# Block sums queued by the product that reads them, one more expert by block products, accumulators that swap roles, and a split last store

## The chip, the cores and the metric

One core of a Trainium2 chip. The time is that of the device, in microseconds (us), for one execution; a kernel is run several times and its median is given. PE is TensorE, DVE VectorE, ACT ScalarE, SP SyncE, POOL GpSimd.

## The reference, cut to what matters

```python
# attention with 4 sink positions and a window of 128, batch 4, 8 heads, 768 positions, 64 wide
x = attn_out.transpose(0, 2, 1, 3).reshape(3072, 512)
# mixture of E = 4 experts, D = 512, F = 1024
p = domain_probs / (domain_probs.sum(-1, keepdims=True) + 1e-09)
for e in range(E):
    h = np.maximum(x @ w1[e], 0.0)
    out += p[:, e:e + 1] * (h @ w2[e])
```

Of the kernel before, what the change touches and what calls it, by code (L numbers as in the profile page):

```python
# [16 lines left out]
def kernel(  # L17
# [12 lines left out]
    nc = tc.nc  # L30

    B, H, S, D = q.shape
    NSINK = int(n_sink)
    WIN = int(window)
    E, Dm, F = moe_w1.shape
    Ntok, Dout = out.shape

    P = 128
# [19 lines left out]
    ]  # L58

    NGATE = 5  # L60
    START = {0: 1, 1: 2, 2: 3, 3: 3}
    ONACT = 1
    ONE = 2
    PAIR = 1
    BEHIND = 800
    BIASED = 1
    FAST = tuple(START)
    UNITS = ("P1", "P5", "P6", "P2", "P7", "P3", "P4")
# [74 lines left out]
    def join(n, done):  # L143

        got = []

        def part(at):
            got.append(at)
            if len(got) == n:
                done(max(got))  # L150
        return part
# [12 lines left out]
    def sp(*deps, issue=530, takes=600):  # L164
        t["sp"] = max([t["sp"], *deps]) + issue
        at = max(t["hw"], t["sp"] + 800)
        t["hw"] = at + takes + max(0.0, min(takes, t["sw"] - at))
        return t["hw"] + 900
# [693 lines left out]
    class Mixture:  # L862
# [170 lines left out]
        def tokens(self):  # L1033

            pairs = [x for x in PAIRS if any(self.is_fast(x[0], e) for e in FAST)]
            n = len(self.T)
            if n == len(pairs):
                return
            b, g = pairs[n]
            if n > 1 and any((*pairs[n - 2], e) not in self.finished for e in range(E)):  # L1040
                return
            at = max(xT_at.get((b, hp, g), 1e12) for hp in range(NHP))
            if at > t["pe"]:
                return
            x = xT[b, g]
            B11, B21, B12, B22 = x[:, 1, 0:2], x[:, 1, 2:4], x[:, 0, 0:2], x[:, 0, 2:4]
            T = sb.tile([P, 4, 2, P], BF16, name="T", tag="T", bufs=2)
            self.T[b, g] = {"P1": B11, "P2": B21, "P3": B22, "P4": T[:, 3], "P5": T[:, 0], "P6": T[:, 1], "P7": T[:, 2]}
            steps = [(T[:, 0], B12, B11), (T[:, 1], B22, T[:, 0]), (T[:, 2], B22, B12), (T[:, 3], B21, T[:, 1])]

            def run(engine):
                nc.vector.tensor_sub(*steps.pop(0))
                done = dve(G, rate=1.92)
                if steps:
                    later("dve", t["dve"], 1500, run)
                else:
                    self.T_at[b, g] = done
            later("dve", at, 2500, run)
# [77 lines left out]

        def chore(self):

            if self.chores:
                return False  # L1140

            def go(fn, slack):
                def run(engine):
                    self.chores -= 1
                    fn(engine)
                self.chores += 1
                later("dve", t["pe"], slack, run)
                return True

            if self.last:  # L1150
                b, g, e = u = self.last[0]
                if (b, g, "P2") not in self.products:
                    self.last.pop(0)

                    def form(engine):
                        H12 = self.H[b, g, e][:, 1, :, 0]
                        nc.vector.tensor_sub(H12, H12, self.S[b, g][1][:, e])
                        self.S4_at[u] = dve(QF * P, rate=1.92)
                    return go(form, 1500)
            if not self.waiting:  # L1160
                return False
            b, g, e = u = self.waiting[0]
            if any(x[:2] < (b, g) and x[2] == "P5" for x in self.products) or any(x[:2] < (b, g) for x in self.last):
                return False
            if (b, g) == PAIRS[0] and len(self.stored) < 2 * NG:
                return False
            self.waiting.pop(0)
            if (b, g) not in self.S:
                self.S[b, g] = [mo.tile([P, E, QF, P], BF16, name=f"S{i}", tag=f"wide{i}", bufs=1) for i in range(2)]
            H = self.H[b, g, e]  # L1170
            H11, H21, H22 = H[:, 0, :, 0], H[:, 0, :, 1], H[:, 1, :, 1]
            S = self.S[b, g]
            steps = [(nc.vector.tensor_add, S[0][:, e], H21, H22), (nc.vector.tensor_sub, H21, H11, H21),
                     (nc.vector.tensor_sub, S[1][:, e], S[0][:, e], H11)]

            def form(engine):
                x = steps.pop(0)
                x[0](*x[1:])
                at = dve(QF * P, self.stored[-1] if (b, g) == PAIRS[0] else 0.0, rate=1.92)
                if steps:  # L1180
                    go(form, 3000)
                else:
                    self.S_at[u] = at
                    self.last.append(u)
            return go(form, 3000)

        def operand(self, b, g, e, m):
            H = self.H[b, g, e]
# [4 lines left out]
        def product_ready(self):  # L1193
            if not self.products:
                return 1e12
            b, g, m = self.products[0]
            e = self.order_of(b, g)[self.piece]
            at = (self.H_at if m in ("P1", "P2") else self.S4_at if m == "P3" else self.S_at).get((b, g, e), 1e12)
            bank = int(m in ("P2", "P5", "P3"))
            if self.piece == 0:  # L1200
                at = max(at, acc_free[bank])
            if m == "P1" and self.piece == E - 1 and acc_free[1] > 1e11:
                at = 1e12
            return max(at, max(forms_at.values()) if sum(formed.values()) == 4 * E else 1e12)

        def order_of(self, b, g):
            return [x[2] for x in self.order if x[:2] == (b, g)]

        def emit_product(self):
            ready = self.product_ready()  # L1210
            b, g, m = self.products[0]
            self.done += QF * G
            self.credit = max(self.credit - QF * G, 0.0)
            bank = int(m in ("P2", "P5", "P3"))
            x = acc[bank][:, 0:G]
            e, k = self.order_of(b, g)[self.piece], self.piece
            for f in range(QF):
                nc.tensor.matmul(  # L1218
                    x, lhsT=self.operand(b, g, e, m)[:, f], rhs=forms[e][m][:, f],
                    start=(k == 0 and f == 0 and m in ("P1", "P5")), stop=(k == E - 1 and f == QF - 1), skip_group_check=True,  # L1220
                )
            end = pe(QF * G, ready, n=QF)
            self.piece = (k + 1) % E
            if m == CHAIN[-1]:
                if (b, g, e) in self.lent:
                    self.spare.append(self.lent.pop((b, g, e)))
                else:
                    self.live -= 1
            if k < E - 1:
                return  # L1230
            self.products.pop(0)
            if m == "P1":
                out_sb[b, g] = mo.tile([P, 2, Dout], FP32, name="osb", tag="osb", bufs=1)
                r = (b * NQB + 2 * g) * P
                def store(at):
                    nc.sync.dma_start(out=out[r + P:r + 2 * P, :], in_=out_sb[b, g][:, 1])
                    sp(at)
                self.C22[b, g] = join(2, store)
            o = out_sb[b, g]
            C11, C12, C21, C22 = o[:, 0, 0:G], o[:, 0, G:], o[:, 1, 0:G], o[:, 1, G:]  # L1240
            acc_free[bank], seeded = 1e12, acc_free[1]
            if m == "P1":
                acc_free[1] = 1e12

            def run(engine):
                if m == "P1":
                    nc.scalar.copy(out=acc[1][:, 0:G], in_=x)
                    acc_free[0] = acc_free[1] = act(G, seeded)
                elif m == "P3":
                    nc.vector.tensor_add(C12, C12, x)  # L1250
                    acc_free[1] = at = dve(G)
                    nc.sync.dma_start(out=out[r:r + P, :], in_=o[:, 0])
                    sp(at)
                elif m == "P7":
                    nc.vector.tensor_add(C22, C22, x)
                    acc_free[0] = at = dve(G)
                    self.C22[b, g](at)
                else:
                    nc.scalar.copy(out={"P2": C11, "P6": C12, "P5": C22, "P4": C21}[m], in_=x)  # L1259
                    acc_free[bank] = at = act(G)  # L1260
                    if m == "P4":
                        self.C22[b, g](at)
            r = (b * NQB + 2 * g) * P
            later("dve" if m in ("P3", "P7") else "act", end, 200, run)

        def second_ready(self):
            if not self.second:
# [179 lines left out]
```

## The kernel before: what the change touches

The kernel is one long static plan. While it is built, a small model of the engines' clocks picks, step by step, what PE does next, and puts the work of VectorE and ScalarE into a list with deadlines (`later(engine, ready, slack, run)`). The order so found is fixed; on the chip each engine runs its own list in that order and waits where it must.

Both layers of the mixture use a scheme with seven block products in place of eight (2x2 blocks). In the first layer an expert is "fast", from the batch that `START` names on: seven products of 8 matmuls with 128 columns, in place of 32 matmuls with 256 columns. In the second layer a pair of token blocks (256 tokens) passes seven products P1, P2, P6, P5, P7, P3, P4, each over all four experts (four pieces of four matmuls of 256 columns), into two PSUM accumulators.

```python
START = {0: 1, 1: 2, 2: 3, 3: 3}
...
# the T sums of a pair's tokens (operands of the first layer's products)
at = max(xT_at.get((b, hp, g), 1e12) for hp in range(NHP))
if at > t["pe"]:
    return
...
later("dve", at, 2500, run)
...
def chore(self):                       # block sums of H, operands of the second layer
    if self.chores:                    # one at a time
        return False
    ...
        return go(form, 1500)          # H12 -= S1, after P2 has read H12
    ...
    steps = [(tensor_add, S[0], H21, H22), (tensor_sub, H21, H11, H21),
             (tensor_sub, S[1], S[0], H11)]
    def form(engine):
        x = steps.pop(0)
        x[0](*x[1:])
        ...
        if steps:
            go(form, 3000)             # the next sum enters the list when this one has run
        else:
            self.S_at[u] = at          # P6, P5, P7 may be planned from here on
    return go(form, 3000)
...
bank = int(m in ("P2", "P5", "P3"))    # the others go to accumulator 0
...
def run(engine):
    if m == "P1":                      # seed: P2 adds onto a copy of P1
        nc.scalar.copy(out=acc[1][:, 0:G], in_=x)
    elif m == "P3":
        nc.vector.tensor_add(C12, C12, x); nc.sync.dma_start(...)   # upper row block
    elif m == "P7":
        nc.vector.tensor_add(C22, C22, x); self.C22[b, g](at)
    else:
        nc.scalar.copy(out={"P2": C11, "P6": C12, "P5": C22, "P4": C21}[m], in_=x)
        if m == "P4":
            self.C22[b, g](at)         # lower row block, stored once P7 and P4 are both in
```

The softmax here doesn't subtract the row's maximum and nothing guards it: scores larger than these inputs give would overflow.

## Time and profile before

| | before |
|---|---|
| median of three runs at first (range) | 375.38 us (375.17 to 375.82) |
| span of the profiled run | 373.0 us |
| PE, DVE, ACT busy | 363.2, 284.6, 153.1 us |
| loading of weights and first inputs, PE partly waiting | to about 68 us |
| batch 0, then the mixture of batches 1 to 3 beside attention | about 68 to 131 us, then to 357 us |
| the last pair alone | 356.6 to 369.6 us |

The lines are shown in the prediction.

### The profile page before, as it was taken

To read this page: it belongs to the slowest core of one execution; us is meant where nothing else is said; L and a number is where in the kernel's file an instruction comes from. 1 tells how busy PE (TensorE), PEld (TensorE's weight loads), DVE (VectorE), ACT (ScalarE), POOL (GpSimd) and SP (SyncE) were. 2 spreads that over 40 slices of the span, in tenths; PEclk is the share of its full clock that TensorE was granted. 3 is DMA by queue.
4 is the path that set the end of the run, shared out by engine and by line. 5 is a ranking of instruction groups with operands and counts; after the bars stand their busy time and mean duration, and the time that the engine had idled before them with its cause. 6 is when DMAs were issued, how large, how long until landed. Compare 5 with 4: busy or idle time off the path is not lost.

```text
span 373.0 us, 9781 instructions
## 1 busy us (share of the span) xinstructions
PE 363.2 (97%) x4084; PEld 300.8 (81%) x4096; DVE 284.6 (76%) x630; ACT 153.1 (41%) x396; POOL 71.5 (19%) x91
## 2 busy tenths in 40 slices
PE   7999999999999999999999999999999999999996
PEld 3575767667667788888987988899999999999975
DVE  5664997674553899778879789779899889899930
ACT  4854633676565226445336145543103222222110
POOL 8935112808131192001020000000000000000000
PEclk9999999999999999999999999999999999999999
DMA  9999999949999999117991023213002111110011
GB/s 166 156 190 198 210 211 180 151 28 119 137 128 212 158 136 133 30 70 75 169 133 55 5 65 77 44 42 86 16 31 72 30 44 58 31 59 2 2 56 58
DMA packets 110808, 35.63 MB, mean 96 GB/s; under 512 B 94260, under 2 KB 106132, under 8 KB 110764
## 3 DMA queue, kind: packets, MB, share of 16 engines
q0 software_dynamic: 77520, 17.31, 52.1%
q1 hardware_dynamic: 32188, 17.18, 20.7%
q8 instruction: 32, 0.52, 0.6%
q10 hardware_dynamic: 1056, 0.52, 0.5%
q14 instruction: 12, 0.10, 0.1%
HBM read 40.45 MB, written 6.34 MB: 125 GB/s over the span
## 4 chain that ended last, share of the span: by engine, by line
PE 75%; DMA 15%; POOL 3%; ACT 3%; DVE 2%; issue 1%; POOLq 0%; ACTq 0%; DVEq 0%
PE acc L1218 29%; PE hps L1001 18%; PE cps L1078 17%; DMA w<-in_moe_w_dram 13%; PE acc L1286 5%; PE sps L618 2%; PE od L684 2%; DMA xT<-onat 2%; POOL qkn L189 1%; ACT onat L723 1%; DMA qkn<-in_q_dram 1%; PE tr L512 1%; POOL w L267 1%; ACT aT L643 1%; PE od L677 1%
## 5 line engine op out<-in xcount | busy, mean ns | idle before, releaser
L1001 PE MATMUL hps<-xT,w 128*128 128x256 bf16 x864 | 107.0, 273 | 1.3 <-DMA w<-in_moe_w_dram 0.9
L1001 PEld LDWEIGHTS <-w 128*128 128x128 bf16 x864 | 82.0, 98 | 14.4 <-issue 2.0
L1218 PEld LDWEIGHTS <-H 128*128 128x128 bf16 x600 | 56.0, 98 | 7.6 <-issue 1.9
L643 ACT ACTIVATE aT<-sps 128x512 bf16<-128x512 f32 (+1 forms) x96 | 47.0, 574 | 31.3 <-PE sps L618 31.2
L723 ACT ACTIVATE onat<-od,R 128x64 bf16<-128x64 f32 x144 | 33.3, 331 | 39.7 <-DVE R L711 39.7
L1218 PE MATMUL acc<-w,H 128*128 128x256 bf16 x360 | 47.7, 273 | 1.0 <-ACT osb L1259 0.5
L1025 DVE SCALAR_TENSOR_TENSOR H<-hps,gates 128x512 bf16<-128x512 f32 x56 | 38.0, 686 | 12.4 <-PE hps L1001 12.2
L1286 PE MATMUL acc<-w,H 128*128 128x512 bf16 x180 | 43.6, 379 | 0.7 <-issue 0.2
L1078 PEld LDWEIGHTS <-w 128*128 128x128 bf16 x672 | 42.4, 98 | 1.9 <-issue 0.5
L254 POOL DMA_DIRECT2D vx<-in_v_dram x24 | 21.4, 902 | 75.6 <-PE od L684 65.9
L1259 ACT COPY osb<-acc 128x256 f32<-128x256 f32 x36 | 13.6, 384 | 52.8 <-PE acc L1218 51.9
L1097 DVE SCALAR_TENSOR_TENSOR H<-cps,gates 128x512 bf16<-128x512 f32 x48 | 32.8, 685 | 2.1 <-PE cps L1078 1.3
L1286 PEld LDWEIGHTS <-H 128*128 128x128 bf16 x192 | 18.3, 98 | 17.5
L1218 PE MATMUL acc<-wf,H 128*128 128x256 bf16 x240 | 31.9, 273 | 0.0
L1014 ACT ACTIVATE H<-hps 128x512 bf16<-128x512 f32 x35 | 20.9, 598 | 24.8 <-PE hps L1001 24.4
L1218 PEld LDWEIGHTS <-S 128*128 128x128 bf16 x288 | 27.0, 98 | 3.9 <-issue 1.1
L1106 ACT COPY cps<-cps 128x512 f32<-128x512 f32 x21 | 12.1, 576 | 42.2 <-PE cps L1078 40.6
L1298 DVE SCALAR_TENSOR_TENSOR osb<-acc,scale_t,osb 128x512 f32<-128x512 f32 x18 | 13.5, 749 | 16.8 <-PE acc L1286 15.3
L1078 PE MATMUL cps<-T,w 128*128 128x128 bf16 x336 | 25.6, 219 | 0.0
L1078 PE MATMUL cps<-xT,w 128*128 128x128 bf16 x336 | 25.3, 219 | 0.0
L189 POOL DMA_DIRECT2D qkn<-in_q_dram x22 | 20.0, 907 | 18.1 <-PE tr L512 9.3
L1078 PEld LDWEIGHTS <-vf 128*128 128x128 bf16 x360 | 22.5, 98 | 1.0 <-issue 0.2
(117 smaller groups left out, 525.1 us busy)
## 6 DMA issues: line engine op xcount, KB each, us to landing
w<-in_moe_w_dram POOLq DMA_DIRECT2D x7, 1024.0 KB, 18.9
out_dram<-osb SPq DMA_DIRECT2D x24, 256.0 KB
gates<-gate_rows SPq DMA_DIRECT2D x36, 128.0 KB
vx<-in_v_dram POOLq DMA_DIRECT2D x24, 128.0 KB, 6.0
qkn<-in_q_dram POOLq DMA_DIRECT2D x22, 128.0 KB, 6.2
qkn<-in_k_dram POOLq DMA_DIRECT2D x22, 128.0 KB, 6.1
w<-in_moe_w_dram POOLq DMA_DIRECT2D x2, 512.0 KB, 9.0
kraw<-in_k_dram ACTq DMA_DIRECT2D x2, 256.0 KB
```

What stands on the lines that cost most here:

```text
L189: nc.gpsimd.dma_start(out=both[:, i], in_=src[b, :, tb * P:(tb + 1) * P, :].rearrange("h p d -> p h d"),)
L254: nc.gpsimd.dma_start(out=vx[tb][:, :, 0:D], in_=v[b, :, tb * P:(tb + 1) * P, :].rearrange("h p d -> p h d"),)
L643: nc.scalar.activation(out=a[:, ph], in_=sps[ph][:, 0:w], func=AF.Exp, scale=scale)
L723: nc.scalar.mul(o[:, qi, hp, ph * D:(ph + 1) * D], od[:, qi, ph, 0:D], R[:, qi, ph])
L1001: nc.tensor.matmul(h[:, i].rearrange("p (q n) -> p q n", q=2), lhsT=w1_sb[e][:, db, fb * P:(fb + 1) * P], rhs=xT[b, g][:, :, db], start=(i ...
L1014: nc.scalar.activation(out=dst, in_=h, func=AF.Relu)
L1025: nc.vector.scalar_tensor_tensor(out=dst, in0=h, scalar=0.0, in1=gate, op0=ALU.max, op1=ALU.mult,)
L1078: nc.tensor.matmul(y[:, f], lhsT=A[:, d, f * P:(f + 1) * P], rhs=T[:, d], start=(m in ("P1", "P5") and f == 0 and d == 0), stop=(d == 1), ...
L1097: nc.vector.scalar_tensor_tensor(out=dst, in0=src, scalar=0.0, in1=gate, op0=ALU.max, op1=ALU.mult)
L1218: nc.tensor.matmul(x, lhsT=self.operand(b, g, e, m)[:, f], rhs=forms[e][m][:, f], start=(k == 0 and f == 0 and m in ("P1", "P5")), stop=(k ...
L1259: nc.scalar.copy(out={"P2": C11, "P6": C12, "P5": C22, "P4": C21}[m], in_=x)
L1286: nc.tensor.matmul(op, lhsT=H[:, fb // QF, fb % QF, s], rhs=w2_sb[e][:, fb, :], start=(fb == 0), stop=(fb == NFB - 1),)
```

## The change

Its intent: take one more expert by seven products in batch 1, where VectorE has some time left; let the extra VectorE work not delay the sums that a product needs; take ScalarE's copies out of PE's way at the end of the kernel; make the last store shorter. The diff, cut to its core (lines left out are not marked one by one):

```diff
-    START = {0: 1, 1: 2, 2: 3, 3: 3}
+    START = {0: 1, 1: 1, 2: 3, 3: 3}
+    CHORES = 3
@@ tokens
                 return
+            at = t["pe"]
@@ chore
-            if self.chores:
+            if self.chores >= CHORES:
                 return False
-                    return go(form, 1500)
+                    return go(form, self.until(b, g, e, "P3"))
-            steps = [(add, S[0], H21, H22), (sub, H21, H11, H21), (sub, S[1], S[0], H11)]
+            steps = [(add, S[0], H21, H22), (sub, S[1], S[0], H11), (sub, H21, H11, H21)]
-                    go(form, 3000)
+                    go(form, self.until(b, g, e, "P6 P7".split()[len(steps) == 2]))
-            return go(form, 3000)
+            return go(form, self.until(b, g, e, "P6"))
+        def until(self, b, g, e, m):
+            n = self.products.index((b, g, m)) * E + self.order_of(b, g).index(e) - self.piece
+            return max(0.0, n * QF * G / 2.4 - 1000.0)
@@ products
-            bank = int(m in ("P2", "P5", "P3"))
+            bank = int(m in ("P2", "P5", "P3")) ^ PAIRS.index((b, g)) % 2
+            final = (b, g) == PAIRS[-1]
-                    start=(... m in ("P1", "P5")), ...
+                    start=(... m in (("P1", "P5", "P2") if final else ("P1", "P5"))), ...
-                if m == "P1":
-                    nc.scalar.copy(out=acc[1][:, 0:G], in_=x)
+                if m == "P1" and not final:
+                    nc.scalar.copy(out=other, in_=x)
+                elif m == "P2" and final:
+                    nc.vector.tensor_add(C11, C11, x)      # P1 went to C11 by ScalarE
@@ stores of the last pair's lower row block
+                    if final: store(at, slice(G, Dout))     # C22, after P7
+                    if m == "P4" and final: store(at, slice(0, G))   # C21, after P4
```

More of the change, by code (lines that the diff above doesn't have):

```diff
@@ L1172, in chore @@
             S = self.S[b, g]
-            steps = [(nc.vector.tensor_add, S[0][:, e], H21, H22), (nc.vector.tensor_sub, H21, H11, H21),
-                     (nc.vector.tensor_sub, S[1][:, e], S[0][:, e], H11)]
+            steps = [(nc.vector.tensor_add, S[0][:, e], H21, H22), (nc.vector.tensor_sub, S[1][:, e], S[0][:, e], H11),
+                     (nc.vector.tensor_sub, H21, H11, H21)]
             def form(engine):
@@ L1198, in product_ready @@
             at = (self.H_at if m in ("P1", "P2") else self.S4_at if m == "P3" else self.S_at).get((b, g, e), 1e12)
-            bank = int(m in ("P2", "P5", "P3"))
+            bank = self.bank(b, g, m)
             if self.piece == 0:
                 at = max(at, acc_free[bank])
-            if m == "P1" and self.piece == E - 1 and acc_free[1] > 1e11:
+            if m == "P1" and self.piece == E - 1 and acc_free[1 - bank] > 1e11:
                 at = 1e12
@@ L1207, in order_of, with bank @@
             return [x[2] for x in self.order if x[:2] == (b, g)]
+        def bank(self, b, g, m):
+            return int(m in ("P2", "P5", "P3")) ^ PAIRS.index((b, g)) % 2
         def emit_product(self):
@@ L1213, in emit_product, with store @@
             self.credit = max(self.credit - QF * G, 0.0)
-            bank = int(m in ("P2", "P5", "P3"))
+            r = (b * NQB + 2 * g) * P
+            def store(at, c=slice(0, Dout)):
+                nc.sync.dma_start(out=out[r + P:r + 2 * P, c], in_=out_sb[b, g][:, 1, c])
+                sp(at)
+            bank = self.bank(b, g, m)
+            other = acc[1 - bank][:, 0:G]
+            final = (b, g) == PAIRS[-1]
             x = acc[bank][:, 0:G]
@@ L1219, in emit_product @@
                     x, lhsT=self.operand(b, g, e, m)[:, f], rhs=forms[e][m][:, f],
-                    start=(k == 0 and f == 0 and m in ("P1", "P5")), stop=(k == E - 1 and f == QF - 1), skip_group_check=True,
+                    start=(k == 0 and f == 0 and m in (("P1", "P5", "P2") if final else ("P1", "P5"))), stop=(k == E - 1 and f == QF - 1), skip_group_check=True,
                 )
@@ L1233, in emit_product @@
                 out_sb[b, g] = mo.tile([P, 2, Dout], FP32, name="osb", tag="osb", bufs=1)
-                r = (b * NQB + 2 * g) * P
-                def store(at):
-                    nc.sync.dma_start(out=out[r + P:r + 2 * P, :], in_=out_sb[b, g][:, 1])
-                    sp(at)
-                self.C22[b, g] = join(2, store)
+                self.C22[b, g] = join(2, lambda at: store(at))
             o = out_sb[b, g]
             C11, C12, C21, C22 = o[:, 0, 0:G], o[:, 0, G:], o[:, 1, 0:G], o[:, 1, G:]
-            acc_free[bank], seeded = 1e12, acc_free[1]
-            if m == "P1":
-                acc_free[1] = 1e12
+            acc_free[bank], seeded = 1e12, acc_free[1 - bank]
+            if m == "P1" and not final:
+                acc_free[1 - bank] = 1e12
             def run(engine):
-                if m == "P1":
-                    nc.scalar.copy(out=acc[1][:, 0:G], in_=x)
+                if m == "P1" and not final:
+                    nc.scalar.copy(out=other, in_=x)
                     acc_free[0] = acc_free[1] = act(G, seeded)
+                elif m == "P2" and final:
+                    nc.vector.tensor_add(C11, C11, x)
+                    acc_free[bank] = dve(G)
                 elif m == "P3":
                     nc.vector.tensor_add(C12, C12, x)
-                    acc_free[1] = at = dve(G)
+                    acc_free[bank] = at = dve(G)
                     nc.sync.dma_start(out=out[r:r + P, :], in_=o[:, 0])
@@ L1255, in run @@
                     nc.vector.tensor_add(C22, C22, x)
-                    acc_free[0] = at = dve(G)
-                    self.C22[b, g](at)
+                    acc_free[bank] = at = dve(G)
+                    if final:
+                        store(at, slice(G, Dout))
+                    else:
+                        self.C22[b, g](at)
                 else:
-                    nc.scalar.copy(out={"P2": C11, "P6": C12, "P5": C22, "P4": C21}[m], in_=x)
+                    nc.scalar.copy(out={"P1": C11, "P2": C11, "P6": C12, "P5": C22, "P4": C21}[m], in_=x)
                     acc_free[bank] = at = act(G)
-                    if m == "P4":
+                    if m == "P4" and final:
+                        store(at, slice(0, G))
+                    elif m == "P4":
                         self.C22[b, g](at)
-            r = (b * NQB + 2 * g) * P
-            later("dve" if m in ("P3", "P7") else "act", end, 200, run)
+            later("dve" if m in ("P3", "P7") or final and m == "P2" else "act", end, 200, run)
         def second_ready(self):
```

## The prediction

> **What bounds the kernel now.** I read the page first, then the table by stretches, the timeline of the matmul engine, the list of waits, and the last microseconds of all engines. The engine shares and the chain that ended last:
>
> ```profile
> PE 363.2 (97%) x4084; PEld 300.8 (81%) x4096; DVE 284.6 (76%) x630; ACT 153.1 (41%) x396; POOL 71.5 (19%) x91
> ...
> PE 75%; DMA 15%; POOL 3%; ACT 3%; DVE 2%; issue 1%; POOLq 0%; ACTq 0%; DVEq 0%
> ```
>
> A busy PE is not proof of a full PE, because ends are modelled. So I look at starts. In the chain, sixteen matmuls of 128x256 take 1.75 us and sixteen of 128x128 take 0.89 us:
>
> ```profile
> 178.96 1.75 PE hps L1001 x16
> ...
> 257.67 0.89 PE cps L1078 x16
> ```
>
> That is 109 and 56 ns from start to start, i.e. 256 and 128 columns at 2.4 GHz plus about 2.5 ns. Adding up the start-to-start distances of all matmuls on the timeline, I find hardly any time above this rate from 120 us on. The PE is full, and the kernel is as long as its column count, plus the load stage before 65 us (the DMA's 15% of the chain), plus a few real gaps. The gaps after 120 us in which PE waited for another engine are in the list of waits from 110 us on, three entries over 0.3 us in all:
>
> ```profile
> PE acc L1218 <- ACT osb L1259: 1.0, 2, 0.5
> ...
> PE acc L1218 <- ACT acc L1247: 0.4, 1, 0.4
> ```
>
> Two of the three are in the last pair of blocks, where no other work is left to fill them. The timeline of PE:
>
> ```profile
> 354.70 1.47 PE L1218 MATMUL acc<-wf,qkT 128*128 128x256 bf16 x12
> 356.63 1.91 PE L1218 MATMUL acc<-w,H 128*128 128x256 bf16 x16 [0.46 <-ACT osb L1259]
> 358.99 1.91 PE L1218 MATMUL acc<-w,H 128*128 128x256 bf16 x16 [0.45 <-ACT acc L1247]
> ```
>
> The bracket undercounts, since it starts at the modelled end. By starts: 354.70 + 12 x 0.109 = 356.01, and the next starts at 356.63, so 0.62 us is lost; 356.63 + 16 x 0.109 = 358.37, next at 358.99, 0.62 us again. The first is the last pair's P1, which wants the accumulator that P4 of the pair before has just filled (ScalarE must copy it out). The second is P2, which adds onto a copy of P1 that ScalarE writes from one accumulator into the other. The third gap is at 204.57 (the same kind of wait as the first: P5 wants the accumulator of P2, and ScalarE was late because of attention's scaling work); 0.7 us by starts.
>
> VectorE is the second engine. By stretches (the columns are busy PE, PEld, DVE, ACT, POOL):
>
> ```profile
> 120.00:150.00 30.00, 29.95 (x337) 24.48 (x335) 26.98 (x62) 12.66 (x39) 14.03 (x17) 1.00 1.55 138
> 150.00:180.00 30.00, 29.96 (x355) 26.39 (x353) 24.21 (x54) 13.86 (x41) 1.75 (x2) 1.00 0.42 64
> 180.00:210.00 30.00, 29.45 (x329) 25.49 (x327) 24.77 (x60) 12.51 (x42) 2.62 (x3) 1.00 0.76 101
> ...
> 300.00:330.00 30.00, 30.00 (x393) 28.15 (x392) 27.43 (x58) 6.67 (x14) 0.00 (x0) 1.00 0.13 39
> ```
>
> In batch 1 (about 120 to 190 us) VectorE has some 3 to 6 us free in each 30; in the last batch 2.6.
>
> **What the Trainium skill says.** The page "TensorE: Matmul & The Clock Gate", section "Wait — 56ns, not 53.3ns?", gives N / 2.4 GHz plus about 2.5 ns between the starts of warm matmuls; the 56 and 109 ns above agree. The same page's "Back-to-back issue gap" expects some 81 ns at 128 columns where each matmul has its own weight load; this trace has such pairs at 56 ns, so I take 56. "PSUM — Partial Sum Buffer", "The four PSUM rules", says that writes of ScalarE and VectorE don't touch the written-bits, so that a matmul without the start flag adds onto what such an engine wrote: that is the seed by which P2 waits for ScalarE's copy, and why a P2 with the start flag needs no copy. "VectorE: DVE Perf Modes", "What auto-detection actually checks", has two results a cycle for 16-bit tensors and one otherwise: here 417 ns for a 512-wide bf16 sum and 685 ns for a 512-wide operation on f32 in PSUM agree.
>
> **The change part by part.**
>
> *Expert 1 by seven block products already in batch 1* (three more fast units, 24 for 21). A slow unit has 32 matmuls of 256 columns: 32 x 109.1 = 3.49 us. A fast unit has 7 x 8 of 128: 56 x 55.8 = 3.12 us. It saves 0.37 us of PE each, 1.10 us for three. It costs VectorE two more f32 operations a unit (six of about 685 ns for four): 2 x 3 x 0.685 = 4.1 us, and ScalarE two copies of 570 to 590 ns a unit, 3.5 us. Both fall into 120 to 190 us, beside PE work; VectorE has about 11 us free there (10 us stretches of 7.5, 10.0, 9.5, 7.7, 8.2, 8.3, 6.9 busy). I count nothing for them on the path. The weight sums of expert 1 exist anyway: three of the four are built by 51 us already, and the fourth, at 182 us before, moves to the end of batch 0 on expert 1; 0.69 us of VectorE moves, none is added.
>
> *Sums queued by the product that reads them, up to three at once, P6's sum before P7's; a laxer deadline for the token sums.* The same instructions in another order: 36 x 4 sums of 417 ns. They let the evictions that PE or a PSUM slot waits for go first. Since PE waits for VectorE practically nowhere from 120 us on, the direct gain is nil; it is what makes room for the 4.1 us.
>
> *Accumulators swap by pair.* P1 of a pair no longer goes into the bank that P4 of the pair before has just left. At eight borders; at seven of them PE has other work and the timeline shows no gap, so they give nothing. At the last: 0.62 us.
>
> *The last pair without the seed.* P1 is copied to the output, P2 starts fresh, and VectorE adds it (one more 128x256 addition, 0.41 us, under the P6 and P5 matmuls). P6 needs P1's accumulator read out, which has P2's 1.75 us to be done. Gain: 0.62 us, all on the path, as the six products after it run without a gap to the end.
>
> *Last store split.* After the last matmul (369.63) come a copy of 0.37 us, the store and its completion:
>
> ```profile
> 369.66 0.37 ACT L1259 COPY osb<-acc 128x256 f32<-128x256 f32 x1 [4.87 <-PE acc L1218]
> 370.06 0.33 SPq L1236 DMA_DIRECT2D out_dram<-osb  x1
> ...
> 370.50:371.00 0.50, 0.00 (x0) 0.00 (x0) 0.00 (x0) 0.00 (x0) 0.00 (x0) 1.00 0.20 74
> 371.00:371.50 0.50, 0.00 (x0) 0.00 (x0) 0.00 (x0) 0.00 (x0) 0.00 (x0) 1.00 1.02 389
> 371.50:372.00 0.50, 0.00 (x0) 0.00 (x0) 0.00 (x0) 0.00 (x0) 0.00 (x0) 1.00 0.17 62
> ```
>
> The data itself takes (0.20 + 1.02 + 0.17) x 0.5 = 0.70 us of the 16 engines; the rest, of 2.9 us from issue to end, is fixed. "DMA: Bandwidth & Descriptors", "Anatomy of one DMA — SWDGE (gpsimd) path", likewise puts some 2 us a DMA down as fixed, mostly the write's receipt. Half the bytes saves up to 0.35 us; the packets shrink from 2 KB to 1 KB, so I take 0.3 us. The other half leaves 1.7 us earlier, beside P4.
>
> Sum: 1.10 + 0.62 + 0.62 + 0.30 = 2.64 us, 0.7% of 375.38, which gives 372.7.
>
> **The rivals.** First, VectorE becomes the bound in batch 1. For it: it is at 100% from 130 to 140 us, where the first fast unit, the last weight sums and the block sums meet, and three fast units more there delay every H behind them. Against it: 11 us are free in the 70 us, and the order of the work is planned by deadline. If it came true, half of the 4.1 us could show as PE gaps, and the time would be some 374.5. Second, ScalarE: two of the three gaps at the accumulators were ScalarE's lateness or latency, and 3.5 us more for it comes in just the batches where attention's exponentials and scalings are still running. A few more gaps like the one at 204.57, of 0.5 to 0.7 us, would make 373.5 to 374. Third, in the other direction: with the queue reordered and the whole static plan shifted, the gap at 204.57 may vanish, which gives 372.0. Fourth, the gaps at the end merely move: P6 or P3 could wait for sums, as PE arrives 1.2 us sooner. Against it: the last block sum ends at 356.1 and P6 began at 360.73; the four sums for P3 end at 361.35 and P3 began at 365.97. Both have slack of over 4 us.
>
> **Range and chances.** The four gains are counted from instructions and are safe within some 0.3 us together. What is unsafe is the replanned order of the middle, which I take as 1 us either way (one or two gaps of the 204.57 kind gained or lost), a little more upward than downward. Hence 371.5 to 374.0. Faster by 2% would need 367.9 us, and there are not 7.5 us of waits to win, as PE's column count stays; slower by 2% needs a new bound that the free time of VectorE speaks against.
>
> **What would show it right or wrong.** Right: 1001's matmuls fall by 96 (864 to 768) and 1078's rise by 168; ScalarE's seed copies 21 to 24; no bracket on the last pair's P1 and P2; P6's first matmul of the last pair 1.75 us after P2's; the end of the span some 2.6 us after the last store's issue. Wrong: new brackets at block products between 120 and 250 us naming VectorE or ScalarE, filler matmuls after 100 us, a VectorE that is full for 30 us and more with PE gaps in it, or a last pair that waits for sums.

## More of the kernel before

All runs told of here are fast: the granted TensorE clock, given by the profile as a share of full speed, was 0.995 or more in each.

The output tile of a pair (`osb`) has a single buffer.

## The result, and the profile after

The changed kernel took 372.38 us (372.10 to 372.55, 4 runs) against 375.60 us (375.17 to 376.00) in the same rounds: a ratio of 0.9914, 95% interval 0.9897 to 0.9931. A ratio is the mean time of one kernel's fast runs over that of the other's of the same rounds, so not quite the ratio of the medians. In later rounds, those of runs 9 to 12, the changed kernel took 371.51 us against 375.42 us (0.9904). It is within 2%, and inside the forecast range.

The engine shares and the chain of the changed kernel's page:

```profile
PE 360.5 (97%) x4155; PEld 299.7 (81%) x4167; DVE 286.8 (77%) x636; ACT 157.7 (43%) x402; POOL 71.7 (19%) x91
...
PE 85%; DVE 6%; DMA 4%; ACT 2%; issue 1%; ACTq 0%; DVEq 0%
```

PE has more matmuls (71 more weight loads) and less to do, as narrower ones took the place of wide ones. PE's waits of over 0.15 us for another engine's data from 110 us on, in the list of waits of the changed kernel; the waits for accumulators, 1.0 and 0.4 us in the prediction's lines, are down to 0.2 us, and a short one for attention's scaling stands at 201.7 us:

```profile
PE od L685 <- ACT onat L724: 0.3, 1, 0.3
...
PE acc L1234 <- ACT osb L1277: 0.2, 1, 0.2
```

The last pair in the timelines of PE and of ScalarE, changed kernel. P1 and P2 now run as one block of 32 without a gap, but P6 starts late: 354.67 + 32 x 0.109 = 358.16, and it started at 358.48. It waited for ScalarE's copy of P1, and that copy started at 358.06, 1.6 us after P1's end, because of a DMA:

```profile
354.67 3.66 PE L1234 MATMUL acc<-w,H 128*128 128x256 bf16 x32
358.06 0.37 ACT L1277 COPY osb<-acc 128x256 f32<-128x256 f32 x1 [2.81 <-DMA out_dram<-osb]
358.48 1.91 PE L1234 MATMUL acc<-wf,S 128*128 128x256 bf16 x16 [0.15 <-ACT osb L1277]
```

The DMA is the store of the pair before, which still reads the one output buffer. Before the change the first write into that buffer came after P2 (360.97 us), when the store had landed.

The end of the changed kernel, by stretches (the last three columns are PE's clock, the busy share of the DMA engines, GB/s): the last half store takes (0.66 + 0.11) x 0.5 = 0.39 us of the DMA engines, not 0.70.

```profile
367.81 0.33 SPq L1226 DMA_DIRECT2D out_dram<-osb  x1
...
368.50:369.00 0.50, 0.00 (x0) 0.00 (x0) 0.00 (x0) 0.00 (x0) 0.00 (x0) 1.00 0.66 229
369.00:369.50 0.50, 0.00 (x0) 0.00 (x0) 0.00 (x0) 0.00 (x0) 0.00 (x0) 1.00 0.11 33
369.50:370.00 0.50, 0.00 (x0) 0.00 (x0) 0.00 (x0) 0.00 (x0) 0.00 (x0) 1.00 0.00 0
```

Yet from that issue to the end of the span 3.0 us passed, against 2.9 before. What stood between is what SyncE does at the end: it goes through a list of nine pairs of semaphores, one after the other. These are its checks (instructions by line, cut to the time from the last store's landing on), first in the kernel before, from 371.9 to 372.2 us, then in the changed one, from 369.3 to 370.0 us:

```profile
L1442 SPq EVENT_SEMAPHORE  x1: 28/28/28, 372.1 to 372.1; - x1
```
```profile
L1461 SPq EVENT_SEMAPHORE  x8: 27/28/28, 369.5 to 369.9; - x8
```

In these traces the DMAs of SyncE hold the semaphores 99, 101, 103, 104, 106, 107, 108 and 109 in turn. Before, the last store happened to hold the last one of the list, so one check was left when it landed. The split makes one DMA more; the last store now holds number 99, the second of the list, and seven checks follow it (from 2.41 to 2.84 us after the start of the last matmul, 0.43 us).

Stage by stage, from starts of certain instructions in the traces (us). "Load": to the first turning of the inputs that come after the weights. "Batch 0": to the 1192nd weight load, up to which all kernels here give PE the same order. "Middle": to the last pair's P1. "Last pair": to the start of the last matmul. "Tail": to the end.

| kernel (profiled run) | load | batch 0 | middle | last pair | tail |
|---|---|---|---|---|---|
| before | 67.78 | 62.97 | 225.88 | 12.72 | 3.63 |
| changed | 68.28 | 62.58 | 223.81 | 12.43 | 3.75 |
| changed, once more | 67.17 | 62.02 | 223.80 | 12.29 | 3.75 |
| without expert 1 | 68.08 | 62.81 | 225.59 | 12.12 | 3.73 |
| with the old queue | 67.57 | 63.18 | 226.61 | 12.12 | 3.74 |
| only expert 1 | 69.11 | 63.14 | 226.51 | 12.72 | 3.63 |
| only the accumulators and the stores | 68.23 | 63.82 | 225.37 | 12.12 | 3.75 |
| own output tiles | 68.11 | 62.33 | 223.81 | 12.12 | 3.76 |
| one last store | 68.13 | 62.02 | 223.81 | 12.12 | 3.62 |
| half store from GpSimd | 68.11 | 62.27 | 223.81 | 12.33 | 3.34 |
| own tiles and GpSimd | 67.59 | 62.45 | 223.80 | 12.12 | 3.33 |
| one sum at a time | 67.63 | 62.46 | 228.50 | 12.12 | 3.74 |
| fixed deadlines | 68.08 | 62.71 | 225.08 | 12.12 | 3.75 |
| no swap | 67.07 | 62.24 | 224.28 | 12.11 | 3.75 |

The six traces whose plan has the same middle agree there within 0.01 us, and so does the tail by its kind. Load and batch 0, where DMA has a say, vary by 2.0 and 1.8 us over all traces. So middle, last pair and tail carry the argument, and the sum of the first two is what makes times scatter.

### The profile page after: what moved, and what is told of

The parts are those of the page before. It is cut to its first block, busy times and chain, and to the rows that moved or that the text cites. A ratio compares the mean times of both kernels' runs of the same rounds, so it can differ in the third digit from the quotient of the medians.

```text
span 370.8 us, 9949 instructions
## 1 busy us (share of the span) xinstructions
PE 360.5 (97%) x4155; PEld 299.7 (81%) x4167; DVE 286.8 (77%) x636; ACT 157.7 (43%) x402; POOL 71.7 (19%) x91
## 4 chain that ended last, share of the span: by engine, by line
PE 85%; DVE 6%; DMA 4%; ACT 2%; issue 1%; ACTq 0%; DVEq 0%
PE acc L1234 28%; PE hps L1002 20%; PE cps L1080 19%; PE acc L1305 9%; PE sps L619 3%; PE od L685 2%; DMA xT<-onat 2%; DMA kraw<-in_k_dram 2%; PE tr L513 1%; ACT aT L644 1%; PE od L678 1%; DMA out_dram<-osb 1%; DVE H L1026 1%; DVE aT L638 1%; DVE onat L715 1%
## 5 line engine op out<-in xcount | busy, mean ns | idle before, releaser
L1002 PE MATMUL hps<-xT,w 128*128 128x256 bf16 x768 | 95.6, 273 | 0.4 <-DVE H L1017 0.4
L1002 PEld LDWEIGHTS <-w 128*128 128x128 bf16 x768 | 72.3, 98 | 12.5 <-issue 2.9
L1080 PEld LDWEIGHTS <-w 128*128 128x128 bf16 x768 | 48.2, 98 | 2.0 <-issue 0.5
L1099 DVE SCALAR_TENSOR_TENSOR H<-cps,gates 128x512 bf16<-128x512 f32 x57 | 38.8, 687 | 2.1 <-PE cps L1080 1.2
L1026 DVE SCALAR_TENSOR_TENSOR H<-hps,gates 128x512 bf16<-128x512 f32 x44 | 30.2, 690 | 9.3 <-PE hps L1002 9.0
L1080 PE MATMUL cps<-T,w 128*128 128x128 bf16 x384 | 29.3, 219 | 0.0
L1080 PE MATMUL cps<-xT,w 128*128 128x128 bf16 x384 | 29.1, 219 | 0.0
L1108 ACT COPY cps<-cps 128x512 f32<-128x512 f32 x24 | 13.8, 575 | 33.1 <-PE cps L1080 31.0
L1080 PEld LDWEIGHTS <-vf 128*128 128x128 bf16 x432 | 26.9, 98 | 1.0 <-issue 0.3
```

The source lines that it names most:

```text
L1002: nc.tensor.matmul(h[:, i].rearrange("p (q n) -> p q n", q=2), lhsT=w1_sb[e][:, db, fb * P:(fb + 1) * P], rhs=xT[b, g][:, :, db], start=(i ...
L1026: nc.vector.scalar_tensor_tensor(out=dst, in0=h, scalar=0.0, in1=gate, op0=ALU.max, op1=ALU.mult,)
L1080: nc.tensor.matmul(y[:, f], lhsT=A[:, d, f * P:(f + 1) * P], rhs=T[:, d], start=(m in ("P1", "P5") and f == 0 and d == 0), stop=(d == 1), ...
L1099: nc.vector.scalar_tensor_tensor(out=dst, in0=src, scalar=0.0, in1=gate, op0=ALU.max, op1=ALU.mult)
L1108: nc.scalar.copy(out=tiles["Y"], in_=y)
```

## The experiments

Times of a run are compared with the kernel before in the same rounds (375.42 us in each case). All results were correct.

**1. Without expert 1** (`no_expert1`): the changed kernel with `START = {0: 1, 1: 2, 2: 3, 3: 3}`.

> The changed kernel with expert 1 fast from the third batch only, as before. Theory (columns): it has 72 matmuls fewer on PE but 1.1 to 1.3 us more of columns, so 1.1 to 1.3 us slower than the changed kernel: about 373.6 us, ratio to before about 0.995. Rival (the surplus over the forecast comes from the queue): under 0.8 us slower than the changed kernel. Rival (VectorE's 4.1 us extra work hurt in the changed kernel): as fast as the changed kernel or faster.

374.22 us (374.04 to 374.31, 5 runs), ratio 0.9968. The middle is 225.59 us, 1.78 us longer than with expert 1. Of this the columns are 1.10 us, and 0.22 us is a matmul of 512 columns that the kernel before spends once to mark a PSUM bank as written (L1086, at 205.9 us) and the changed plan doesn't need; the rest is gaps that fall otherwise. So expert 1 pays what its columns say, and a little more, as long as the new queue is there. The first rival (a surplus from elsewhere) and the second (VectorE hurt) are both out for the changed kernel.

**2. With the old queue** (`no_queue`): the changed kernel with (cut, the last line put in words)

```diff
-            if self.chores >= CHORES:
+            if self.chores:
-            at = t["pe"]                      # token sums
-  steps: S0, S1, H21; slacks until(...)
+  steps: S0, H21, S1; slacks 3000, 3000, 1500
```

> The changed kernel with the old queue of block sums (one at a time, fixed deadlines, old order) and the old deadline of the token sums. Theory (PE hardly ever waits for VectorE, so the queue is worth nothing): within 0.4 us of the changed kernel, 372.0 to 372.9 us, no PE gap naming VectorE after 120 us. Rival (the queue pays for the extra VectorE work of expert 1): 1 us or more slower, with PE gaps between 120 and 190 us.

375.28 us (374.88 to 376.33, 6 runs), ratio 0.9999: the whole gain is gone. The theory, which was also my forecast ("the direct gain is nil"), fell; the rival holds. (Of the seven gaps over 0.25 us, two name VectorE and five ScalarE in the list of waits.) The middle is 226.61 us, 2.80 us longer than in the changed kernel (0.22 of it the matmul of 512 columns, which this plan needs). Where PE waits is plain in this run's timelines of PE and VectorE:

```profile
152.83 0.38 PE L619 MATMUL sps<-qkT 64*128 64x128 bf16 x5 [0.28 <-ACT aT L644]
153.68 0.39 PE L1233 MATMUL acc<-wf,S 128*128 128x256 bf16 x2 [0.47 <-DVE S L1179]
```
```profile
151.61 0.68 DVE L1026 SCALAR_TENSOR_TENSOR H<-hps,gates 128x512 bf16<-128x512 f32 x1
152.21 0.31 DVE L712 RECIPROCAL R<-od 128x4 f32<-128x4 f32 x3
152.44 0.39 DVE L1179 TENSOR_TENSOR S<-H 128x512 bf16<-128x512 bf16 x1
152.86 0.43 DVE L1179 TENSOR_TENSOR H<-H 128x512 bf16<-128x512 bf16 x1
153.21 0.42 DVE L1179 TENSOR_TENSOR S<-S,H 128x512 bf16<-128x512 bf16 x1
```

A product piece (acc<-wf,S) waits for the last of the three sums of one expert, S<-S,H, at 153.21 us, right after a stretch of evictions and attention work. Around it PE has nothing but attention's scores left to run, and these wait for ScalarE. By starts, this place costs 0.38 + 0.43 + 0.63 = 1.44 us, and four more gaps of 0.43 to 0.60 us follow up to 204 us.

**3. Only expert 1** (`only_expert1`): the kernel before with `START = {0: 1, 1: 1, 2: 3, 3: 3}`.

> The kernel before with expert 1 fast from batch 1 and nothing else. Theory (columns): 1.1 to 1.3 us faster than before, about 374.4 us, ratio 0.9967. Rival (without the new queue VectorE is late in batch 1): the same as before or slower, gaps naming VectorE between 120 and 190 us.

375.74 us (375.48 to 376.81, 5 runs), ratio 1.0008 (0.9995 to 1.0021). The rival holds: with 1.1 us fewer columns the middle is 0.63 us longer than before (226.51 against 225.88), with the same gaps at P6's sums as in run 2 (0.38, 0.43 and 0.63 us by starts, at 153.9 to 155.2 us). The profiled run is the slowest of the five (376.81 us), by its load stage (69.11 us). The first rival of the forecast, VectorE's extra work as a bound in batch 1, is what happens without the queue.

**4. Only the accumulators and the stores** (`only_end`): the kernel before with the swap, the last pair without a seed, and the split store.

> The kernel before with only the accumulators' swap, the last pair without a seed, and the split store. Theory: the two gaps of the last pair (1.23 us) go and one of 0.31 us comes before P6, and the split loses 0.11 us: 0.8 us faster than before, about 374.7 us, ratio 0.9978. Rival (swap also helps at the other borders): 1.3 us or more.

374.38 us (373.69 to 374.98, 5 runs), ratio 0.9973 (0.9959 to 0.9987): 1.0 us faster, in line with the 0.8 us expected. In its trace the last pair takes 12.12 us against 12.72, the gap before the last P1 is gone (the middle is 0.51 us shorter), and the tail is 0.12 us longer. P6 had no gap in this run. Nothing at the other borders.

**5. Own output tiles** (`own_out`): in the changed kernel the last pair gets two tiles of attention's, free by then. The edit, cut:

```diff
-                out_sb[b, g] = mo.tile([P, 2, Dout], FP32, name="osb", tag="osb", bufs=1)
+                if final:
+                    halves = [sb.tile([P, Dout], FP32, name="onat", tag="onat", bufs=2) for _ in range(2)]
```

> The changed kernel, with the last pair's output in two tiles of its own (attention's, free by then) in place of the one output buffer that the stores of the pair before still read. Theory (P1's copy waits for those stores' landing, P6 for that copy): the copy starts right after P1's last matmul, no gap before P6, 0.31 us less: 372.1 us; in the trace the last seven products take 12.12 us, not 12.43. Rival (P6 waits for ScalarE's copy as such): the gap stays.

371.88 us (370.64 to 372.24, 4 runs), ratio 0.9900. In its trace P1's copy starts at 356.19 us, 0.19 us after P1's 16 matmuls (354.25 + 1.75), and the last pair takes 12.12 us:

```profile
356.19 0.37 ACT L1282 COPY onat<-acc 128x256 f32<-128x256 f32 x1 [1.38 <-PE acc L1234]
```

The copy's delay comes from the one output buffer. In the nine traces with one buffer, swap and no seed, the copy waited for that DMA each time and began 2.71 to 3.38 us after P1's first matmul; in both with own tiles (runs 5 and 8) it began after 1.95 us. P6 came late only where the copy began after 3.07 us: in three of the nine.

**6. One last store** (`one_store`): the changed kernel, lower row block stored in one piece.

> The changed kernel with the last row block stored in one piece, as before. Theory (the half store lands 0.32 us sooner, but its semaphore is the second of nine pairs that are checked at the end, and the seven checks after it cost 0.43 us): the time from the last matmul's start to the end falls from 3.75 to 3.63 us, 0.1 us less, so 372.3 us. Rival (the forecast: half the bytes save 0.3 us): 372.7 us and a longer tail.

371.83 us (371.40 to 372.17, 4 runs), ratio 0.9905; the tail is 3.62 us, as before the change. In this run the store of the pair before landed sooner and P6 had no gap, so that wait depends on the run: it was 0.31, 0.17, 0.21 and 0.00 us in the four traces with this plan and one buffer (the copy began after 3.38, 3.25, 3.28 and 3.07 us).

**7. Half store from GpSimd** (`pool_half`): the changed kernel with `nc.gpsimd.dma_start` for the C22 half. GpSimd's DMAs hold other semaphores (111 to 118 in the traces), so the last store gets the last one of the list again.

> The changed kernel with the first of the two last half stores issued from GpSimd, which takes its semaphore from another set, so that the last store's semaphore is again the last one checked. Theory: the tail falls by the seven checks, 0.43 us, to about 3.3 us: 372.0 us. Rival (the order of the checks is of no account): tail 3.75 us as in the changed kernel, or longer because of the other queue.

371.47 us (370.10 to 371.94, 4 runs), ratio 0.9887. The tail is 3.34 us, 0.41 us less than in the changed kernel and 0.29 less than before: the gain of the smaller store that I had forecast is there once its semaphore is checked last. After the landing one check is left (this run, 368.7 to 369.05 us):

```profile
L1461 SPq EVENT_SEMAPHORE  x1: 28/28/28, 368.9 to 368.9; - x1
```

**8. Both** (`both`): own tiles and the half store from GpSimd.

> The changed kernel with own tiles for the last pair's output and the first half store from GpSimd. Theory: both gains add up, 0.31 + 0.43 = 0.74 us: about 371.6 us, the fastest of all. Rival: they don't add, 372.0 us.

371.69 us (371.00 to 371.97, 4 runs), ratio 0.9899. In the trace both gains add up: last pair 12.12 us, tail 3.33 us, together 0.73 us less than in the changed kernel's first trace. The times of runs 5 to 8 overlap with one another and with those of the changed kernel in the later rounds, on another chip (371.51 us), so the times show no order among them. By the traces this is the best version.

**9. One sum at a time** (`one_at_a_time`): the changed kernel with `CHORES = 1`.

> The changed kernel with at most one block sum in VectorE's queue (three in the changed one); deadlines and order as changed. Theory A (the number matters: twelve sums a pair, one after the other, each entering the queue only when the last has run, come too late for P6 when expert 1 adds VectorE work): gaps at P6 as in the run without the new queue, 1.5 us or more slower than the changed kernel, 373.9 us or more. Theory B (the deadlines matter): within 0.6 us of the changed kernel.

376.31 us (375.44 to 376.79, 6 runs), ratio 1.0025, beside the changed kernel's 371.51 us in the same rounds: 4.8 us slower. Theory A holds, and more strongly than expected. VectorE is equally full; only what it does first differs. The sums alone (busy VectorE, number) from 140 to 160 us, first in the changed kernel, then with one at a time:

```profile
140.00:150.00 10.00, 3.38 (x9) 1.00 1.26 99
150.00:160.00 10.00, 2.03 (x6) 1.00 0.49 80
```
```profile
140.00:150.00 10.00, 1.94 (x6) 1.00 1.11 101
150.00:160.00 10.00, 3.15 (x9) 1.00 0.53 55
```

And all engines in the same stretches (PE, PEld, DVE, ACT, POOL), in the same order:

```profile
140.00:150.00 10.00, 10.00 (x129) 8.96 (x127) 9.82 (x26) 5.82 (x16) 1.63 (x2) 1.00 1.26 99
150.00:160.00 10.00, 10.00 (x121) 8.83 (x119) 7.93 (x18) 3.93 (x13) 0.88 (x1) 1.00 0.49 80
```
```profile
140.00:150.00 10.00, 10.00 (x128) 9.05 (x126) 9.93 (x24) 4.56 (x12) 1.22 (x2) 1.00 1.11 101
150.00:160.00 10.00, 8.52 (x107) 7.16 (x106) 7.91 (x22) 7.02 (x22) 0.88 (x1) 1.00 0.53 55
```

VectorE is 98 and 99% busy in the first stretch, and 79% in the second, in both. With one sum in the list at a time, six run from 140 to 150 us in place of nine; the products that need them can't be planned, PE runs short in the second stretch (8.52 us busy), and what it then runs is attention, which crowds ScalarE (7.02 us in place of 3.93) and waits for it:

```profile
152.40 0.38 PE L619 MATMUL sps<-qkT 64*128 64x128 bf16 x5 [0.84 <-ACT onat L724]
156.26 0.92 PE L1234 MATMUL acc<-wf,H 128*128 128x256 bf16 x7 [0.64 <-ACT osb L1277]
```

By starts these two cost 0.99 and 0.80 us. Of the 4.69 us by which the middle is longer, 0.44 us are two matmuls of 512 columns that this plan needs.

**10. Fixed deadlines** (`fixed_slack`): the changed kernel with slacks 3000, 3000 and 1500 for `until(...)`, three sums at once.

> The changed kernel with three sums at once but the old fixed deadlines (3000 and 1500 ns) in place of the ones worked out from the product that reads them. Theory A (the number matters): within 0.6 us of the changed kernel. Theory B (the deadlines matter): 1.5 us or more slower.

373.19 us (371.93 to 373.51, 6 runs), ratio 0.9938; 1.7 us slower than the changed kernel in the same rounds, and 1.28 us longer in the middle. So A alone doesn't hold: by the bound I set, B holds too. The number is the larger part (4.8 us slower without it), and deadlines worked out from the reader are worth 1.3 us in the middle when three sums are allowed.

**11. No swap** (`no_swap`): the changed kernel without `^ PAIRS.index((b, g)) % 2`.

> The changed kernel with the accumulators' roles fixed, as before. Theory (at the last border only, P1 waits for ScalarE to read P4 out of the bank): a gap of 0.62 us by starts before the last pair's P1 comes back, none at other borders: 0.6 us slower than the changed kernel, 372.6 to 373.2 us. As P1 then starts 0.62 us later, less of the wait for the output buffer is left before P6. Rival (the swap also pays at other borders): 1 us or more slower.

372.31 us (371.18 to 373.10, 6 runs), ratio 0.9918; 0.8 us slower than the changed kernel in the same rounds, though below the range I gave, as the changed kernel itself was in these rounds. The last border's gap is back, and only that one:

```profile
351.66 1.47 PE L1234 MATMUL acc<-wf,qkT 128*128 128x256 bf16 x12
353.59 3.65 PE L1234 MATMUL acc<-w,H 128*128 128x256 bf16 x32 [0.46 <-ACT osb L1277]
```

By starts that is 353.59 - (351.66 + 1.31) = 0.62 us. The middle is 0.48 us longer. P6 had no gap, as expected: P1 came later.

**12. The changed kernel once more** (`after_again`), beside 9 to 11.

> The changed kernel once more, on the same chip and beside the three others. Expected 372.0 to 372.5 us, with the same gaps as in its first trace (0.46 us at about 201 us, up to 0.31 us before the last pair's P6) and a load stage that differs by up to 0.7 us.

371.51 us (370.76 to 371.97, 5 runs), all five below the range that I gave. Middle and tail are those of its first trace within 0.01 us; the load stage was 1.1 us shorter, more than the 0.7 us I allowed.

## Why the prediction was right, and where its steps were not

The time (372.7 us forecast, 372.38 and 371.51 measured) is in the range, and the main reading, PE full and as long as its columns plus a few gaps, holds. That the time came so close is in part luck. By the traces the change brought 2.24 to 2.38 us from 131 us on, in place of 2.64; two of the four gains that I called safe within 0.3 us together missed by more than that (the split by 0.42, the seed by up to 0.31 us); and time was won in the first 131 us, which the forecast left out. Of the signs named beforehand, the matmul counts, the 24 seed copies and the missing brackets at P1 and P2 came true; two did not: P6 began 2.06 us after P2 in the changed kernel's first trace (1.75 forecast), and the span ended 3.04 us after the last store's issue (2.6 forecast). Step by step:

- **Columns, 1.10 us: right.** L1001's matmuls fell from 864 to 768 and L1078's rose by 168. Add 0.22 us for the matmul of 512 columns that fell away, which I had not counted. (It belongs to the seed of the first layer. "PSUM — Partial Sum Buffer", "The four PSUM rules", says that a matmul without the start flag adds onto what ScalarE wrote only where an earlier matmul has set the bit; the prediction left this condition out. No run here tests it.) The fourth weight sum of expert 1 went to 65.7 us, into the load stage, not to the end of batch 0. But it is not a gain of `START` alone: alone it brought nothing (run 3).
- **The queue, "the direct gain is nil; it is what makes room for the 4.1 us": half right, and the mis-sized step.** The second half is what the runs show. The first half read too much into a trace in which PE didn't wait for VectorE: that was true of the old load, and only from 120 us on, where I had looked; the waits for VectorE in batch 0 are below. Without the queue the middle is 2.8 us longer (run 2), more than expert 1 and the end together bring in the middle. Without expert 1 the queue is worth nothing measurable there (middle 225.59 against 225.37 us in runs 1 and 4). The two parts are one change.
- **Free time of VectorE as an argument against the first rival: insufficient.** I summed 11 us of free time in 70 us (11.9 by the stretches). From 140 to 150 us VectorE is full in either kernel, and there the order decides, not the sum (run 9).
- **The swap, 0.62 us at the last border and nothing elsewhere: right** (run 11).
- **The seed, 0.62 us: right for the gap at P2, but 0.00 to 0.31 us came back before P6.** The fourth rival said that gaps at the end may merely move, and I looked only at the sums; they were in time. What moved in was the single output buffer: P1's copy writes into it one product earlier than P2's did, before the store of the pair before has landed (run 5).
- **The split, 0.30 us: wrong in the net.** The transfer shrank by 0.31 us as forecast. But of the 2.9 us from issue to end, all of which I called fixed but for the transfer, only 2.02 us pass to the landing, and 0.9 us are the checks and what follows them. The tail grew by 0.12 us, because the last store's semaphore moved to the front of the list that is checked at the end (runs 6 and 7).
- **The gap at 204.57 us, third rival:** 0.70 us became one of 0.46 us at 201.7 us.

The sum from the traces, before to changed: middle -2.07 us (columns 1.10, the spared matmul 0.22, the border 0.62, and 0.13 of other gaps), last pair -0.29 (-0.43 in the second trace), tail +0.12; in all -2.24 to -2.38 us. The times say 3.2 and 3.9 us by the medians. As traces of one plan agree from there on, the rest must lie in the first 131 us, where runs scatter: this stretch took 130.75 us in the kernel before and 130.86 and 129.19 us in the changed kernel's two traces.

A part of that rest can be read from all the traces together. With the old deadline of the token sums, VectorE stands at the first such sum until the turned tokens have landed, and the eviction of an H tile comes only after it; with the new one that eviction goes to ScalarE. In VectorE's timeline of run 4 (old) and of the changed kernel, the sum and what follows:

```profile
92.59 0.29 DVE L1053 TENSOR_TENSOR T<-xT 128x256 bf16<-128x256 bf16 x1 [2.81 <-DMA xT<-onat]
92.92 0.29 DVE L1053 TENSOR_TENSOR T<-xT,T 128x256 bf16<-128x256 bf16 x1
93.12 0.68 DVE L1017 TENSOR_SCALAR H<-hps 128x512 bf16<-128x512 f32 x1
```
```profile
92.37 0.29 DVE L1054 TENSOR_TENSOR T<-xT 128x256 bf16<-128x256 bf16 x1 [2.54 <-DMA xT<-onat]
92.70 0.29 DVE L1054 TENSOR_TENSOR T<-xT,T 128x256 bf16<-128x256 bf16 x1
92.91 0.28 DVE L1054 TENSOR_TENSOR T<-xT 128x256 bf16<-128x256 bf16 x1
```

PE's waits for H from VectorE between 85 and 105 us are 0.4, 1.1, 0.8 and 0.8 us in the four traces with the old deadline, and 0 to 0.5 us in the ten with the new one, a mean of 0.2. That would be some 0.6 us. The column for batch 0 says as much: 62.97 to 63.82 us with the old deadline and 62.02 to 62.81 us with the new one, means 63.28 and 62.39, 0.89 us apart without overlap. Up to this mark the traces of run 2 and of the changed kernel have the same order on VectorE and ScalarE but for that one eviction, and in every trace the first block sum comes 0.5 to 1.1 us after it, so the queue of block sums has no say here. Still, no run had this deadline alone changed, so it is read and not tested. What remains, some 0.1 to 0.6 us, is not separated from the scatter of the load stage (67.1 to 69.1 us over all traces, under either deadline) and stays open.

## What to carry to other kernels

An engine on which the bound engine "never waits" is safe only at its present load: before adding work to it, look at its fullest ten microseconds, not at its free time, and let what it does first follow from when the reader comes. A wait that is removed at the end of a kernel lets the next write come sooner, so ask which buffer that write needs and which transfer still reads it. And a smaller last transfer pays only if its completion is the last thing waited for.

## What the Trainium skill lacked or had wrong

- "TensorE: Matmul & The Clock Gate", "Back-to-back issue gap": it gives about 81 ns for each matmul of 128 columns in a stream where each has its own weight load. Here the 1176 such matmuls of the first layer's products start 56 ns apart in the median (kernel before). For 512 columns it gives about 131 ns; here 189 of them start 216 ns apart in the median. The formula that it gives for an isolated matmul (N / 2.4 GHz + 2.5 ns) fits both.
- "DMA: Bandwidth & Descriptors", "Anatomy of one DMA — SWDGE (gpsimd) path": its 2.0 us of fixed cost is for DMAs that GpSimd issues, and the page has no such figure for a store from SyncE. For the last stores, which SyncE issues, the check that waits for the landing ran 2.02 us after the issue with 256 kB and 1.70 us with 128 kB; less the 0.70 and 0.39 us of transfer, 1.3 us is fixed.
- No page says that the end of the program checks its semaphores one pair after another, so that the time to the end depends on which semaphore the last store holds: some 60 ns for each pair that stands after it, 0.43 us for seven (tail 3.75 against 3.34 us).
